# A 7 x 7 convolution by short transforms: the first weight group taken from one copy of the weights, the second copy loaded later

## The chip, the core and the metric

The kernel runs on one core of a Trainium2 chip. The metric is the device time of one execution, in microseconds (us); the smaller the better. The core has five engines, each with its own instruction queue that is worked off in order: TensorE (PE, with weight loads listed apart as PEld), VectorE (DVE), ScalarE (ACT), GpSimd (POOL) and SyncE (SP), which here only issues DMA transfers. Engines wait for each other by semaphores.

## What is computed

A batch of one image of 224 x 224 pixels with 96 channels (bf16) is convolved circularly with a 7 x 7 kernel from 96 to 96 channels. The reference does it by Fourier transforms over the whole image:

```python
def reference(x, w):                      # x (1,224,224,96), w (7,7,96,96), bf16
    wp = jnp.pad(w, ((0, H - K), (0, W - K), (0, 0), (0, 0)))
    Xf = jnp.fft.rfft2(x.astype(jnp.float32), axes=(1, 2))
    Wf = jnp.fft.rfft2(wp.astype(jnp.float32), axes=(0, 1))
    Yf = jnp.einsum('bhwi,hwio->bhwo', Xf, Wf)
    return jnp.fft.irfft2(Yf, s=(H, W), axes=(1, 2)).astype(jnp.bfloat16)
```

## The kernel before

**Tiles and stages.** The height is cut into 8 blocks of 28 rows, the width into 7 tiles of 32 pixels. Along the height a transform with 17 frequencies `s` is used, along the width the seven taps are summed directly. Four kinds of work go through PE:

- pixels: matmuls of a pixel's rows with the transform matrix `Fm` give `xf` (`a_bank`, `f_jobs`). `jit` then makes sums and differences of `xf` on DVE, called `J`, for a group of three frequencies.
- weights: matmuls with the loaded weights `wq` and a selector matrix `Em` give the transformed weights `WF`. `prep_jobs(gi)` returns the jobs of weight group `gi`; group 0 covers the frequencies 0 and 1, group 1 the frequencies 2 to 4, and so on. A group has 12 jobs; each fills one PSUM bank and is evacuated to `WF` by DVE or ACT. From group 1 on, three jobs on DVE follow (`diff`, the difference of two slots of `WF`).
- rounds: `b_round(t, s, ...)` multiplies `xf` and `J` of tile `t` with `WF` at frequency `s`. Two banks, `b0` and `b1`; ACT copies the first into `tt_`, DVE makes `u` and `v`, POOL or DVE adds them into `yf`, which goes to a scratch in DRAM.
- inverse: matmuls with the matrix `G` bring the scratch of a finished tile back to pixels.

**The weights in `wq`.** A row of `wq` is one of the 49 taps, its columns run over input and output channels. A matmul takes every 96th column, so that it sees one output channel `o` for all input channels. Each tap is loaded twice: row 2k holds tap k from column 0, row 2k+1 the same tap shifted by 48 output channels. One matmul over the 98 rows with both halves of `Em` therefore makes the output channels `o` and `o + 48` together. `Em` lies behind the weights in the same tile, and the columns behind it are zeroed by ACT.

**What sets the order.** Every engine's instructions are chained in the order of the program (`_Ordered`), so the source's order is the order of each queue. `evac` gives an evacuation to DVE or ACT by counts of estimated load. All PSUM tiles come from one pool of eight banks (`bank`), reused in turn; PE waits when the bank eight tiles back isn't evacuated. Within the rounds, side jobs (weight groups, pixels) are dealt out by `add(a, b, jobs)`: the jobs are spread over the half rounds a to b - 1, and `pace` runs those that are due in the middle (`mid`) and at the end (`end`) of a round; for the first rounds the middle of round r is half round 2r, the end 2r + 1.

**The start** is written out by hand. SP loads, in this order: the halo pixels of both halves of the image (`xh`, lines 179 to 180), the first half's pixels (`load_x(0, 0)`), the weights in five column pieces of two transfers each (lines 182 to 187), and the second half's pixels, held behind the second piece. PE runs 8 + 9 warm matmuls on zeros, the halos, the first half's pixels, 2 x 11 more warm matmuls, weight group 0, the second half's pixels; then follow `jit(0, 0)` and, with `g_fin()`, the sine that finishes `G`, and round 0. Lines 707 to 717 of it:

```python
    for n in (11, 11):
        warm(n)
    for f in prep_jobs(0):
        f()
    last = [f() for f in fj[0][1]]
    for jg in range(2):
        for d in load_x(1, jg):
            tc.add_manual_dep(d.ins, last[0].ins.name, SYNC, reason="second tile's pixels later")
    for f in jit(0, 0):
        f()
    g_fin()
```

`g_fin` is returned by `build_g(3)`: POOL makes the angles of `G` in a chain of small dependent operations that stands in its queue behind the masks of `Em` and eight memsets, ACT takes the sine (it is the first instruction of ACT behind the pixels' evacuations and ahead of round 0's `tt_`), POOL multiplies.

Of the kernel before, what the change touches and what calls it, by code (L numbers as in the profile page):

```python
# [46 lines left out]
NWC = 5  # L47
HOLD = 2
# [8 lines left out]
def kernel(  # L57
# [15 lines left out]
    PW2 = 2 * PW  # L73
# [81 lines left out]
    wq = wqx[0:PW2]  # L155
    WC = C * C - C2
    Em = wqx[0:PW2, WC:WC + 2 * NSLOT * NTAP].rearrange("p (h a t) -> p h a t", h=2, a=NSLOT)
# [20 lines left out]
    wsrc = w.rearrange("kh kw i o -> (kh kw) (i o)")  # L178
    for jg in range(2):
        load_rows(xh_bufs[jg], jg, W - PAD, PAD)  # L180
    load_x(0, 0)
    wcut = [WC * c // NWC // 128 * 128 for c in range(NWC)] + [WC]
    wdma = []
    for c0, c1 in zip(wcut, wcut[1:]):
        for k, n in ((PW - 1, 1), (0, PW - 1)):
            wdma.append(dma(wqx[2 * k:2 * (k + n), c0:c1],
                bass.AP(wsrc.tensor, wsrc.offset + k * C * C + c0, [[C * C, n], [C2, 2], [1, c1 - c0]])))
    for d in load_x(0, 1):
        tc.add_manual_dep(d.ins, wdma[2 * HOLD + 1].ins.name, SYNC, reason="second pixels behind the weights")

# [9 lines left out]
    warm(9)  # L200
# [19 lines left out]
    zw = wqx[0:PW2, WC + 2 * NSLOT * NTAP:]  # L220
    SE.copy(out=zw, in_=wu[0:PW2, 0:1].to_broadcast(list(zw.shape)))

    nrj = ftile([R, JG]); pw_i = ftile([R, 1]); aa = ftile([R, NS, 2]); phf = ftile([R, NS, 2]); phe = ftile([R, NS, 2])
    twc = ftile([PW2, KT]); mf = ftile([R, JG, NS * 2])
    iota(nrj[:], [[-B, JG]], base=-1, cm=1)
    iota(pw_i[:], [[0, 1]], cm=1)
# [3 lines left out]
    thp = ftile([R, 1]); qq = ftile([R, JG + 1, NS, 2]); fl = ftile([R, JG + 1, NS, 2])  # L230
# [6 lines left out]
    floor_div(VE, thp[:], pw_i[:], 2 * KT)  # L237
# [9 lines left out]
    SE.activation(out=qq[:], in_=qq[:], func=ACTF.Sin, bias=pi_t[:R, :], scale=-2.0 * math.pi / Q)  # L247
# [8 lines left out]
    iota(twc[:], [[1, KT]])  # L256
    pm = ftile([PW2, 1]); twp = ftile([PW2, 1]); hf = ftile([PW2, 1]); mk = ftile([PW2, NTAP]); mk2 = ftile([PW2, 2, NTAP])
    th14 = ftile([PW2, 1])
    GE.tensor_single_scalar(out=th14[:], in_=thp[0:PW2], scalar=-2.0 * KT, op=ALU.mult)
    GE.tensor_tensor(out=pm[:], in0=th14[:], in1=pw_i[0:PW2], op=ALU.add)  # L260
    floor_div(GE, twp[:], pm[:], 2)
    GE.tensor_single_scalar(out=th14[:], in_=twp[:], scalar=-2.0, op=ALU.mult)
    GE.tensor_tensor(out=hf[:], in0=th14[:], in1=pm[:], op=ALU.add)
    GE.tensor_scalar(out=mk[:, 0:KT], in0=twc[:], scalar1=twp[:, 0:1], scalar2=None, op0=ALU.is_equal)
    GE.tensor_tensor(out=mk[:, KT:NTAP], in0=mk[:, 0:6:2], in1=mk[:, 1:6:2], op=ALU.add)
    GE.tensor_scalar(out=mk2[:, 1], in0=mk[:], scalar1=hf[:, 0:1], scalar2=None, op0=ALU.mult)
    GE.tensor_tensor(out=mk2[:, 0], in0=mk[:], in1=mk2[:, 1], op=ALU.subtract)
    for xb in xh_bufs:
        GE.memset(xb[:, PAD * C:], 0.0)
    for xb in x0_bufs + xn_bufs:  # L270
        GE.memset(xb[:, XW:], 0.0)
    for xb in xf_bufs:
        GE.memset(xb[:, :, :, NS - 1, POS - 1, :].rearrange("c p r j -> c (p r) j"), 0.0)

    VE.tensor_tensor(out=Fm.rearrange("p r s j -> p j s r"), in0=qq[:, 0:JG],
                     in1=mf.rearrange("p j (s r) -> p j s r", r=2), op=ALU.mult)
    qe = qq[0:PW2, JG]
    pe3 = ftile([PW2, NSLOT])
# [4 lines left out]
    for r, k in ((0, KT - 1), (1, 0)):  # L283
        VE.tensor_single_scalar(out=pv[:, NS - 2, r:r + 1], in_=thp[0:PW2], scalar=float(k), op=ALU.is_equal)
    VE.tensor_tensor(out=pv[:, :, 2], in0=pv[:, :, 0], in1=pv[:, :, 1], op=ALU.subtract)
    for k0, k1 in ((0, slot(PGRP[0][1], 0)), (slot(PGRP[0][1], 0), NSLOT)):
        VE.tensor_tensor(out=Em[:, :, k0:k1], in0=pe3[:, k0:k1].unsqueeze(1).unsqueeze(3).to_broadcast([PW2, 2, k1 - k0, NTAP]),
                         in1=mk2[:].unsqueeze(2).to_broadcast([PW2, 2, k1 - k0, NTAP]), op=ALU.mult)
# [51 lines left out]
    def prep_jobs(gi):  # L340
# [3 lines left out]
        ncol = (NSLOT_OF(s0, s1) if full else 2 * ns) * NTAP  # L344
# [4 lines left out]
        def mk_(ob):  # L349
            def f():  # L350
                pw = bank()
                pv_ = pw[:, 0:NB * ncol].rearrange("p (k h q) -> p k h q", h=2, q=ncol)
                ev = Em[:, :, slot(s0, 0):slot(s1 - 1, 2) + 1, :]
                ev = ev.rearrange("p h a t -> p h (a t)") if full else ev.rearrange("p h (s r) t -> p h s (r t)", r=3)[:, :, :, 0:2 * NTAP]
                for k in range(hb):
                    o = ob * hb + k
                    TE.matmul(pv_[:, k], lhsT=wqx[0:PW2, o:o + 127 * C + 1:C], rhs=ev, start=True, stop=True)
                pv_ = pv_[0:C]
                o0, o1 = ob * hb, (ob + 1) * hb
                wv = WF[0:C, slot(s0, 0):slot(s1 - 1, 2) + 1]  # L360
                if full:
                    wv = wv.rearrange("i a t (h o) -> i (a t) h o", h=2)
                    apart(("W", gi), ob, evac(wv[..., o0:o1], pv_.rearrange("i k h q -> i q h k"), NB * ncol))
                    return
# [12 lines left out]

    def NSLOT_OF(s0, s1):
        return slot(s1 - 1, 2) + 1 - slot(s0, 0)
# [320 lines left out]
    for jg in range(2):  # L700
        for f in a_bank(0, xf0, xh_bufs[jg], 0, 3, jg, 0):
            f()
# [209 lines left out]
```

## Time and profile before

Three runs gave 269.27, 269.51 and 270.08 us, median 269.51.

| of the profiled execution | |
|---|---|
| span from the first to the last instruction | 267.8 us |
| median of the runs, which includes what lies around the span | 269.51 us |
| PE busy, 0 to 10.96 us | 9.43 of 10.96 us |
| PE busy, 10.96 to 15.71 us | 4.75 of 4.75 us |
| PE busy, 15.71 to 20.23 us | 4.06 of 4.52 us |
| PE busy, 20.23 to 26.64 us | 6.41 of 6.41 us |
| PE busy, 26.64 to 34 us | 7.22 of 7.36 us |
| PE busy, 34 us to the end | 226.50 of 233.80 us |
| granted clock of TensorE | 1.00 in each of these stretches |

How to read the profile: a timeline line has the start in us, the busy time from first to last of the merged instructions in us, the engine, the source line, the operation, what it writes and reads, the shapes, the count, and in brackets the idle time ahead of it with what ended it. Since all calls go through a helper, all instructions of the kernel carry its line, L89, and are told apart by their tiles. Names of buffers stand without numbers; `ct` are the small tables, `pb` a PSUM bank, `wu` the zeros of the warm matmuls. A matmul's time in a group is its latency; what counts in a stream is the distance from start to start.

### The profile page before, as it was taken

The page shows a single profiled execution, that of the slowest core. Times are in us where ns is not written, and L with a number is a line of the kernel's source. Part 1 is how long each engine was busy: PE and PEld are TensorE (multiplying, and loading weights), DVE is VectorE, ACT ScalarE, POOL GpSimd, SP SyncE. Part 2 cuts the span into 40 slices and gives each one's busy share as a digit, 9 for nine tenths or more (in the row PEclk, how much of TensorE's full clock was granted, in tenths as well). Part 3 has the DMA queues.
Part 4 walks back from the last instruction along what each step waited for, and adds up shares of the span by engine and source line. Part 5 has one row for each costly group of instructions (what it writes and reads, how often), then busy time and mean ns, then how long its engine had stood idle before and what let it go on. Part 6 is the DMA issues. An engine that isn't in the chain of part 4 may idle for free. (4 is left out here: it accounts for less than half of the span.)

```text
span 267.8 us, 12172 instructions
## 1 busy us (share of the span) xinstructions
PE 258.4 (96%) x5144; PEld 237.3 (89%) x5144; DVE 214.3 (80%) x457; ACT 194.6 (73%) x483; POOL 98.9 (37%) x156
## 2 busy tenths in 40 slices
PE   8999999999999999999999999999999999999983
PEld 3679999999999999999999998999999889879862
DVE  5658998889899788779787888787898889878624
ACT  5558988587974577988988789887887854278113
POOL 7782315363656435321422222223222342532100
PEclk9999999999999999999999999999999999999999
DMA  6948011811111498997968487979777624887956
GB/s 169 233 130 213 11 47 46 239 48 72 47 47 50 146 266 143 281 272 199 299 170 241 116 221 235 238 204 329 269 148 216 202 98 154 198 229 186 257 115 206
DMA packets 47014, 46.78 MB, mean 175 GB/s; under 512 B 35286, under 2 KB 37986, under 8 KB 46960
## 3 DMA queue, kind: packets, MB, share of 16 engines
q1 hardware_dynamic: 44672, 43.94, 59.3%
q10 hardware_dynamic: 2288, 2.06, 2.6%
q8 instruction: 40, 0.66, 1.0%
q14 instruction: 14, 0.11, 0.2%
HBM read 24.65 MB, written 21.33 MB: 172 GB/s over the span
## 5 line engine op out<-in xcount | busy, mean ns | idle before, releaser
L89 PE MATMUL pb<-WF,J 96*128 96x96 bf16 x2821 | 162.8, 206 | 1.9 <-DVE J L89 1.1
L89 PEld LDWEIGHTS <-J 96*128 96x128 bf16 x2821 | 138.0, 98 | 12.4 <-issue 3.6
L89 POOL TENSOR_TENSOR yf<-v,u 128x384 bf16<-128x384 f32 x79 | 81.4, 1042 | 146.3 <-issue 84.6
L89 ACT CAST xf<-pb 96x408 bf16<-96x408 f32 (+3 forms) x145 | 67.7, 490 | 9.0 <-PE pb L89 5.4
L89 PE MATMUL pb<-WF,xf 96*128 96x96 bf16 x952 | 59.9, 206 | 0.5 <-ACT xf L89 0.5
L89 DVE TENSOR_TENSOR J<-xf 96x1824 bf16<-96x1824 bf16 (+1 forms) x84 | 56.9, 716 | 0.1
L89 PEld LDWEIGHTS <-xf 96*128 96x128 bf16 x952 | 47.0, 98 | 0.7 <-ACT xf L89 0.6
L89 PE MATMUL pb<-Fm,xn 118*128 118x136 bf16 (+3 forms) x640 | 45.5, 199 | 0.2 <-DVE u L89 0.2
L89 PE MATMUL pb<-tt,Gm 102*84 102x384 bf16 (+1 forms) x132 | 32.7, 326 | 0.4 <-ACT J L89 0.3
L89 ACT CAST WF<-pb 96x480 bf16<-96x480 f32 (+1 forms) x59 | 29.1, 578 | 4.8 <-PE pb L89 4.8
L89 PEld LDWEIGHTS <-xn 118*128 118x128 bf16 x640 | 30.3, 97 | 0.3 <-issue 0.3
L89 ACT CAST J<-pb 84x384 bf16<-84x384 f32 (+1 forms) x64 | 27.7, 490 | 2.6 <-PE pb L89 2.6
L89 ACT CAST yo<-pb 84x384 bf16<-84x384 f32 (+1 forms) x63 | 27.1, 486 | 2.3 <-POOL yf L89 1.3
L89 DVE TENSOR_TENSOR J<-J 96x912 bf16<-96x912 bf16 (+2 forms) x42 | 24.2, 577 | 0.0
L89 PE MATMUL pb<-wq 98*128 98x120 bf16 (+1 forms) x288 | 21.3, 226 | 0.0
L89 PEld LDWEIGHTS <-wq 98*128 98x128 bf16 x288 | 19.6, 151 | 0.2 <-issue 0.2
L89 PE MATMUL pb<-wu 128*128 128x512 bf16 (+1 forms) x75 | 16.8, 385 | 1.1 <-DVE ct L89 1.1
L89 PEld LDWEIGHTS <-wu 128*128 128x128 bf16 (+1 forms) x75 | 8.8, 120 | 8.0 <-issue 2.8
L89 DVE TENSOR_TENSOR yf<-v,u 128x384 bf16<-128x384 f32 x26 | 14.9, 572 | 0.9
L89 PEld LDWEIGHTS <-Gm 102*84 102x84 bf16 (+1 forms) x132 | 11.1, 117 | 1.0 <-issue 0.4
L89 ACT COPY xf<-xf 96x816 bf16<-96x816 bf16 (+3 forms) x20 | 11.3, 633 | 0.0
L89 DVE CAST WF<-pb 96x480 bf16<-96x480 f32 (+1 forms) x13 | 7.5, 609 | 4.2 <-PE pb L89 4.2
(386 smaller groups left out, 234.2 us busy)
## 6 DMA issues: line engine op xcount, KB each, us to landing
scr<-yf SPq DMA_DIRECT2D x30, 288.0 KB
xn<-in_x_dram SPq DMA_DIRECT2D x12, 672.0 KB
tt<-scr SPq DMA_DIRECT2D x24, 336.0 KB
out_dram<-yo SPq DMA_DIRECT2D x12, 252.0 KB
out_dram<-J SPq DMA_DIRECT2D x12, 252.0 KB
tt<-scr SPq DMA_DIRECT2D x6, 288.0 KB
WF<-in_x_dram SPq DMA_DIRECT2D x2, 672.0 KB
out_dram<-tt SPq DMA_DIRECT2D x8, 168.0 KB
```

The source lines that it names most:

```text
L89: r = fn(*a, **k)
```

## The change

The two copies of each tap no longer stand in neighbouring rows. The first copy lies in rows 32 to 80, the second (shifted by 48 output channels) in rows 81 to 127 and, its last two taps, in rows 30 and 31. Weight group 0 uses the first copy alone: 96 matmuls over the rows 0 to 80 with 50 columns instead of 48 over 98 rows with 100 columns; the rows 0 to 31 are zeroed for that. Later groups use all 128 rows as before used 98.

- Loads: first half's pixels, tap 48 in two pieces, the other 48 taps of the first copy, halos, second half's pixels, second copy's first 47 rows; its last two rows follow in the queue when group 0 has read the zeros there, and behind them the second tile's pixels.
- PE: 8 + 8 warm matmuls, first half's pixels, 3 warm matmuls, ten of group 0's twelve jobs, halos, second half's pixels, the last two jobs of group 0.
- Zeros: ACT zeroes 1036 f32 columns behind `Em` and, in rows 0 to 31, columns 0 to 1000 and 1000 to 2300; POOL the columns 2300 to 4608 of these rows, behind the masks.
- Masks: VectorE computes the tap and the copy of a row (`hb`, `ha`, `tap`, `hm`), POOL's four operations for them fall away.
- Rounds: group 1's jobs go to the half rounds 1 and 2 (before 0 and 1), the pixel jobs `fj[1][1]` to 0 to 2 (before 1 to 4).

```diff
-NWC = 5
-HOLD = 2
+FILL = 3
+W1 = 32
+W2 = 30
+ZA = 1000
+ZB = 2300
...
-    PW2 = 2 * PW
+    EP = 128
+    K1 = W1 + PW
+    NU = EP - K1
...
+    def load_w(p, k, n, h):
+        m = (C * C, WC)[h]
+        return dma(wqx[p:p + n, 0:m], bass.AP(wsrc.tensor, wsrc.offset + k * C * C + h * C2, [[C * C, n], [1, m]]))
+
+    load_x(0, 0)
+    m = C * C // 16
+    for a, b in ((0, m // 2), (m // 2, m)):
+        dma(wqx[K1 - 1:K1, 0:C * C].rearrange("p (c m) -> p c m", c=16)[:, :, a:b],
+            bass.AP(wsrc.tensor, wsrc.offset + (PW - 1) * C * C + a, [[C * C, 1], [m, 16], [1, b - a]]))
+    load_w(W1, 0, PW - 1, 0)
     for jg in range(2):
         load_rows(xh_bufs[jg], jg, W - PAD, PAD)
-    load_x(0, 0)
-    wcut = [WC * c // NWC // 128 * 128 for c in range(NWC)] + [WC]
-    wdma = []
-    for c0, c1 in zip(wcut, wcut[1:]):
-        for k, n in ((PW - 1, 1), (0, PW - 1)):
-            wdma.append(dma(wqx[2 * k:2 * (k + n), c0:c1],
-                bass.AP(wsrc.tensor, wsrc.offset + k * C * C + c0, [[C * C, n], [C2, 2], [1, c1 - c0]])))
-    for d in load_x(0, 1):
-        tc.add_manual_dep(d.ins, wdma[2 * HOLD + 1].ins.name, SYNC, reason="second pixels behind the weights")
+    load_x(0, 1)
+    load_w(K1, 0, 32, 1)
+    load_w(K1 + 32, 32, NU - 32, 1)
...
     warm(8)
-    warm(9)
+    warm(8)
...
-    SE.copy(out=zw, in_=wu[0:PW2, 0:1].to_broadcast(list(zw.shape)))
+    def zero_a(rows, c0, c1):
+        SE.copy(out=wz[0:rows, c0:c1], in_=zf[0:rows, 0:1].to_broadcast([rows, c1 - c0]))
+    zero_a(EP, WE // 2 + NSLOT * NTAP, 64 * C)
+    zero_a(W1, 0, ZA)
...
+    zero_a(W1, ZA, ZB)
...
+    VE.scalar_tensor_tensor(out=hm[:, 0:1], in0=hb[:], scalar=-2.0, in1=ha[:], op0=ALU.mult, op1=ALU.add)
+    VE.scalar_tensor_tensor(out=hm[:, 1:2], in0=pw_i[:], scalar=float(PW - W1 + W2), in1=hm[:, 0:1], op0=ALU.is_ge, op1=ALU.subtract)
+    for h in range(2):
+        GE.tensor_scalar(out=mk2[:, h], in0=mk[:], scalar1=hm[:, h:h + 1], scalar2=None, op0=ALU.mult)
+    GE.memset(wz[0:W1, ZB:WE // 2], 0.0)
...
+                if full:
+                    pv_ = pw[:, 0:NB * ncol].rearrange("p (k q) -> p k q", q=ncol)
+                    ev = Em[0:K1, 0, slot(s0, 0):slot(s1 - 1, 2) + 1, :].rearrange("p a t -> p (a t)")
+                    o0 = ob * NB
+                    for k in range(NB):
+                        TE.matmul(pv_[:, k], lhsT=wqx[0:K1, o0 + k:o0 + k + 127 * C + 1:C], rhs=ev, start=True, stop=True)
...
     xf0 = new_xf(0)
-    for jg in range(2):
-        for f in a_bank(0, xf0, xh_bufs[jg], 0, 3, jg, 0):
-            f()
     fj = [f_jobs(0, p) for p in range(3)]
     for p in range(3):
         for f in fj[p][0]:
             f()
-    for n in (11, 11):
-        warm(n)
-    for f in prep_jobs(0):
+    warm(FILL)
+    first_w = prep_jobs(0)
+    for f in first_w[:-2]:
         f()
-    last = [f() for f in fj[0][1]]
     for jg in range(2):
-        for d in load_x(1, jg):
-            tc.add_manual_dep(d.ins, last[0].ins.name, SYNC, reason="second tile's pixels later")
+        for f in a_bank(0, xf0, xh_bufs[jg], 0, 3, jg, 0):
+            f()
+    for f in fj[0][1]:
+        f()
+    for f in first_w[-2:]:
+        f()
+    load_w(W2, NU, W1 - W2, 1)
+    for jg in range(2):
+        load_x(1, jg)
...
     for gi in range(1, len(PGRP)):
-        add(2 * PGRP[gi - 1][0], 2 * PGRP[gi - 1][1] - (2 if gi == 1 else 1), prep_jobs(gi))
+        add(2 * PGRP[gi - 1][0] + (gi == 1), 2 * PGRP[gi - 1][1] - 1, prep_jobs(gi))
...
-            add(1, 5, fj[1][1])
+            add(0, 3, fj[1][1])
```

## The prediction

> **What bounds the kernel now.** I read the page's shares and slices first, then the busy time by stretch, then the timeline of the first 27 us on each engine, the waits, and last the order in which the changed program's instructions stand on each engine.
>
> ```profile
> PE 258.4 (96%) x5144; PEld 237.3 (89%) x5144; DVE 214.3 (80%) x457; ACT 194.6 (73%) x483; POOL 98.9 (37%) x156
> ...
> PE   8999999999999999999999999999999999999983
> ```
>
> TensorE is busy 96% of the span, in every slice. In the stretch from 34 us to the end it is busy 226.5 of 233.8 us, so what it loses before 34 us it can hardly win back. But part of its busy time early on is filler:
>
> ```profile
> 10.96 4.91 PE L89 MATMUL pb<-wu 128*128 128x512 bf16 x22
> ...
> 15.71 3.13 PE L89 MATMUL pb<-wq 98*128 98x100 bf16 x48
> ...
> 20.23 0.51 PE L89 MATMUL pb<-WF,xf 96*128 96x96 bf16 x8 [0.46 <-ACT xf L89]
> ```
>
> From 10.96 to 15.7 us PE multiplies zeros while the weights arrive; then come the first weight group (48 matmuls), the second pixels and, at 20.23, round 0. Meanwhile POOL, ACT and DVE do this:
>
> ```profile
> 7.44 0.31 POOL L89 MEMSET WF<- 118x32 bf16 x4
> ...
> 7.94 0.13 POOL L89 IOTA ct<- 102x1 f32 x1
> 8.16 1.75 POOL L89 TENSOR_SCALAR ct<-ct 102x1 f32<-102x1 f32 x4
> ...
> 10.27 1.08 POOL L89 TENSOR_SCALAR ct<-ct 102x1 f32<-102x1 f32 x4
> ...
> 20.47 0.37 POOL L89 TENSOR_TENSOR ct<-ct,ct 102x84 f32<-102x84 f32 x1
> ...
> 20.88 0.37 ACT L89 ACTIVATE ct<-ct,ct 102x84 f32<-102x84 f32 x1 [0.70 <-POOL ct L89]
> 21.15 0.31 ACT L89 COPY tt__556<-pb 128x192 f32<-128x192 f32 x1
> 21.35 4.23 ACT L89 CAST WF<-pb 96x480 bf16<-96x480 f32 x9
> ...
> 25.61 1.79 DVE L89 TENSOR_TENSOR WF<-WF 96x960 bf16<-96x960 bf16 x3 [0.45 <-ACT WF L89]
> ...
> 26.56 0.47 ACT L89 ACTIVATE tt__670<-pb 128x288 f32<-128x288 f32 x1
> ...
> 26.67 0.34 PE L89 MATMUL pb<-WF,J 96*128 96x96 bf16 x4
> ```
>
> POOL builds matrix G in one dependent chain from 7.94 to 20.84 (20.47 + 0.37). ACT needs its result for one sine, which stands in ACT's queue ahead of round 0's copy `tt_`; ACT already waits 0.70 us for it. From there ACT has no idle time up to 34 us: nine evacuations of weight group 1, two halo copies, then round 1's `tt_`. Group 1 is complete at 25.6, and round 2, which multiplies by it, starts at 26.67. So a second chain, POOL to ACT to group 1 to round 2, runs about even with PE. This is the place to watch.
>
> **PE's own sum.** Removed: 1 of 17 first warm matmuls and 19 of 22 later ones, at 4.91/22 = 0.22 us: 4.4 us. Added: 48 matmuls. The 48 with 100 columns took (3.13 - 0.22)/47 = 62 ns each, start to start; the 32 with 120 columns at 20.58 took 2.17 us, or 63 ns. Since 20 more columns cost 1 ns, the weight read (every 96th element, as after the change) sets the pace, so 50 columns also take 62 ns: 48 x 62 = 3.0 us. Bounds: 35 ns, the pace of the 32 second-pixel matmuls (1.10 us), which have contiguous weights, and 65. The new timetable: warm to 6.5; 96 first-pixel matmuls to 9.4 (3.3 us now for 103, less the 7 halo ones); 3 warm to 10.05; 80 of the 96 to 15.05; 12 halo at 0.06 to 15.8; second pixels 1.1 to 16.9; the last 16 to 17.9; evacuation (0.2 + 0.5) to 18.6. Round 0 would start 1.6 us earlier than 20.23.
>
> **Transfers up to there.** First pixels (0.71 MB) and first copy (0.90 MB) are 1.6 MB; by the trace's DMA packets 1.6 MB had come in by 9.0 us. PE asks for them at 10.05, so this is covered by 1 us. Rows are 18 KB instead of 3.6 KB; the packets of 6,144 bytes moved faster (390 GB/s) than those of 3,584 (240), but the one of 16,384 bytes took 1.38 us; at that pace three rows an engine are 4.1 us and the copy lands near 9.5, still in time. Second pixels and the second copy bring 3.4 MB, by 14 to 16 us. SyncE's queue holds each of these until an earlier one has landed, which moves none past that point. The last two rows are new: they wait for the last of the 96 matmuls (17.9), and the second tile's pixels stand behind them. Small transfers took 1.8 to 2.1 us from issue to landing; with 1.38 for the long row up to 3.4: landed at 20.0 to 21.4. Group 1 wants them at about 20.2, so 0 to 1.2 us, if nothing else holds PE. The next pixels are issued at about 18.5 (now 19.72) and are not late.
>
> **POOL and ACT, the step that decides.** Ahead of G's chain POOL loses four one-column operations (5.06 to 6.14: 1.1 us), does four of the short memsets earlier and gains a memset of 32 x 2308 f32. That shape is not in the trace. 136 columns took 0.21 us and 8 took 0.11, so 0.8 ns a column: 2.0 us. Bounds: 1.0 (two columns at once) and 2.6 (held up by DVE). Masks end at 6.6 instead of 7.50, the memset at 8.6, the remaining short ones at 8.85: G starts 0.9 us later. Against that, its first four operations took 1.75 us where four like them took 1.08: DVE was writing the selector matrix (7.54 to 8.93). After the change that write is over by 8.1, so 0.67 comes back: 8.85 + 12.90 - 0.67 = 21.1. If the hold-up falls on the memset, 21.8. I take 21.3, nearer the first because the eight memsets at 7.44 to 7.98 ran beside the same write and stretched to nothing. The bounds: 20.2 to 21.8.
>
> [...]
>
> ACT is free at about 18.2 and then stands still until 21.3, with round 0's `tt_`, two pixel evacuations and six of group 1 behind the sine. PE fills its eight banks and stops too; so the 1.6 us won are spent waiting. Onward: `tt_` starts 0.27 after the sine (20.88 to 21.15 now): 21.57. From there to the end of round 1's `tt_` took 5.88 us (21.15 to 27.03); three fewer evacuations at 4.23/9 = 0.47 and two more of 320 columns at 0.44: 5.35, so 26.9. Now the new serial piece: in the changed order DVE does `u` of round 1 (0.34), which needs that `tt_`, ahead of the last three evacuations of group 1 (0.6 each); before, all three stood ahead of `u`. 26.9 + 0.35 + 1.8 = 29.05, PE starts round 2 at 29.1 instead of 26.67: **2.4 us late**. From there on the two instruction orders differ in a few evacuations up to about round 5 and then not at all, and PE is the bound: I carry all of it.
>
> The other edits (three VectorE operations for the row masks, ACT's zeroing of 1036, 1000 and 1300 columns by 6.0 us at the pace of 2120 in 1.94) lie under the warm matmuls, which end at 6.5; without that cover they would cost some 0.5 us.
>
> **The sum.** The profiled execution spans 267.8 us; the median of runs is 269.51, 1.7 more, which lies around the span. 267.8 + 2.4 = 270.2 profiled; **271.9 us** as a run's time. From the bounds of POOL (-1.1, +0.5), of the carry and of the evacuations (0.5 either way): 270.3 to 273.0 for this case.
>
> **Rivals.**
> Absorbed: after 34 us PE has 7.3 us of gaps, short waits for DVE and ACT; if half the delay vanishes there, +1.2, 270.7. Against it: these waits move with PE.
> Faster, on the other side: the sine does not hold ACT. Then round 0 at 18.6 plus the present 6.44 us from round 0 to round 2 gives 25.0, plus 0.6 for the two late rows 25.6: 1.0 us early, **268.5**. It decides if POOL's result is there by 18.6; that needs G's chain 2.7 us shorter than the rows say. For it: POOL's spans are rough.
> Transfers: the long rows go at half the pace assumed, the two late rows land at 23.5 and group 1 starts after ACT is free: 1.6 more, 273.5. For it: no row of 18 KB is in the trace.
> No effect: the head's gain and the later sine cancel at round 2 because G's chain starts as now; 269.5.
>
> **How the numbers follow.** Forecast 0.62, absorbed 0.14, faster 0.10, transfers 0.08, no effect 0.06. The likeliest is 271.9. The range 269.9 to 273.5 leaves out the faster case, the case of no effect, and 0.04 above. A difference of 0.3% (0.8 us) is about what a measurement of this kernel can tell from none. Slower: forecast, transfers and 0.11 of the absorbed, 0.81; same 0.09; faster 0.10.
>
> **What would show it.** The first weight group starts near 10 us and round 0 near 18.6; ACT idle some 3 us until a sine at 21 to 22; PE idle in several pieces between 19 and 29; round 2 near 29; the 50-column matmuls 62 ns apart. If the sine comes before 19, or round 2 before 26.7, the forecast is wrong.

## The result and the profile after

The changed kernel takes 273.74 us (median of four runs, 272.65 to 274.23), the kernel before 269.47 us (four runs, 269.27 to 270.08): the ratio is 1.0145, with an interval from 1.0117 to 1.0173. The profiled execution spans 272.4 us, 4.6 more than before. The change costs 4.3 us; the forecast was 2.4. (One run of `g1_chunks` below took 641.29 us at a clock of 1.00 and is in no median.)

The page of the changed kernel, busy time and slices:

```profile
PE 261.8 (96%) x5172; PEld 242.3 (89%) x5172; DVE 215.8 (79%) x462; ACT 197.2 (72%) x485; POOL 99.0 (36%) x153
...
PE   8998899999999999999999999999999999999983
...
PEclk9955999999999999999999999999999999999999
```

PE is as busy as before, 96%. New is the row of the granted clock: two slices at 0.5, where the kernel before had 9 throughout. The record of the clock begins at 7.01 us here and at 5.11 us in the kernel before; ahead of it the warm matmuls start 427 ns apart, behind it some 215. So both executions began at half pace, and the 1.00 that the table of the kernel before gives from 0 us on is that of the recorded part. From there on every change of the clock, in every run, lies a whole number of stretches of 3.41 us behind the last (6.83 us are two of them, 13.65 four). Four of them, with the columns PE, PEld, DVE, ACT, POOL (busy us and instructions), granted clock, DMA share and GB/s:

```profile
7.01:10.43 3.42, 3.42 (x102) 2.94 (x101) 3.17 (x6) 2.30 (x5) 2.90 (x12) 1.00 0.95 218
10.43:13.84 3.41, 3.41 (x56) 3.33 (x55) 1.57 (x3) 1.60 (x4) 2.51 (x13) 1.00 1.17 279
13.84:17.25 3.41, 3.41 (x51) 3.41 (x50) 2.27 (x4) 2.03 (x5) 2.74 (x12) 0.50 1.01 118
...
24.08:27.49 3.41, 3.41 (x44) 3.41 (x42) 1.09 (x2) 3.12 (x7) 0.00 (x0) 0.50 0.86 225
```

From 10.43 to 13.84 PE is never idle (3.41 of 3.41 us), but behind the end of the warm matmuls it has only matmuls of 50 columns; then it runs at half clock for 13.65 us, to 27.49. The timeline of the changed kernel, PE from the first weight group to round 2:

```profile
10.63 5.02 PE L95 MATMUL pb<-wq 81*128 81x50 bf16 x80
15.47 2.23 PE L95 MATMUL pb<-Fm,WF 118*128 118x136 bf16 x25
17.97 1.17 PE L95 MATMUL pb<-Fm,WF 118*128 118x64 bf16 x19 [0.27 <-issue]
18.95 1.13 PE L95 MATMUL pb<-wq 81*128 81x50 bf16 x16
20.83 0.80 PE L95 MATMUL pb<-WF,xf 96*128 96x96 bf16 x8 [0.75 <-DVE WF L95]
...
23.63 3.38 PE L95 MATMUL pb<-wq 128*128 128x120 bf16 x32 [0.34 <-DMA wq<-in_w_dram]
...
31.01 0.34 PE L95 MATMUL pb<-WF,J 96*128 96x96 bf16 x4 [0.50 <-DVE WF L95]
```

Round 0 starts at 20.83, not at 18.6; group 1 waits for its weights and starts at 23.63 (before: 20.58); its 32 matmuls take 3.38 us (before 2.17); round 2 starts at 31.01 (before 26.67). ACT and DVE in the same stretch:

```profile
20.80 0.37 ACT L95 ACTIVATE ct<-ct,ct 102x84 f32<-102x84 f32 x1 [0.68 <-POOL ct L95]
21.67 0.32 ACT L95 COPY tt__585<-pb 128x192 f32<-128x192 f32 x1 [0.50 <-PE pb L95]
...
28.90 0.36 DVE L95 SCALAR_TENSOR_TENSOR u<-pb,tt__692 128x192 f32<-128x192 f32 x1 [1.20 <-ACT tt__692 L95]
29.18 1.77 DVE L95 CAST WF<-pb 96x480 bf16<-96x480 f32 x3
```

The sine comes at 20.80, as before (20.88), and round 0's `tt_` waits for PE, not for the sine. `u` does stand ahead of the last three evacuations of group 1, as the forecast said, but PE waits only 0.50 us for them.

How late PE is against the kernel before, taken at the same matmul of the rounds in both traces: 0.6 us at round 0, 4.34 at round 2, 4.41 at 107 us and 4.41 at 248 us. The loss is made between round 0 and round 2 and carried whole to the end. It splits by the rows: group 1 starts 3.05 us later (23.63 against 20.58), and from its start to round 2 it takes 7.38 us instead of 6.09, of which 1.17 are the 32 matmuls at half clock (23.63 to the next matmuls at 26.81, against 20.58 to 22.59). So the first theory was: thin matmuls drop the clock, and the order on DVE costs the rest; its rivals, that the clock is all of it, and that transfers are. A part of round 0's lateness belongs to the execution and not to the change: half pace at the start lasted to 7.01 us here, with the first pixels at 7.44, and in the runs below to between 3.94 (h2_chunks_early, first pixels at 6.24) and 6.85 us (x_pace, 7.36).

### The profile page after: what moved, and what is told of

The parts are those of the page before. It is cut to its first block, busy times and chain, and to the rows that moved or that the text cites. A ratio compares the mean times of both kernels' runs of the same rounds, so it can differ in the third digit from the quotient of the medians.

```text
span 272.4 us, 12227 instructions
## 1 busy us (share of the span) xinstructions
PE 261.8 (96%) x5172; PEld 242.3 (89%) x5172; DVE 215.8 (79%) x462; ACT 197.2 (72%) x485; POOL 99.0 (36%) x153
## 4 chain that ended last, share of the span: by engine, by line
PE 66%; DVE 13%; POOL 7%; issue 6%; DMA 4%; ACT 3%; DVEq 0%; ACTq 0%; POOLq 0%
PE pb L95 66%; POOL ct L95 5%; DVE J L95 4%; DVE WF L95 3%; DVE v L95 3%; DVE u L95 2%; DMA xf<-scrb 2%; ACT xf L95 1%; DMA wq<-in_w_dram 1%; DVE yf L95 1%; DMA scrb<-yf 1%; POOL yf L95 1%; POOL wq L95 1%; ACT J L95 1%; DVE xf L95 0%
## 5 line engine op out<-in xcount | busy, mean ns | idle before, releaser
L95 PE MATMUL pb<-wq 128*128 128x120 bf16 (+1 forms) x336 | 25.4, 234 | 0.3 <-DMA wq<-in_w_dram 0.3
L95 PEld LDWEIGHTS <-wq 128*128 128x128 bf16 (+1 forms) x336 | 23.6, 154 | 0.7 <-issue 0.5
L95 PE MATMUL pb<-wu 128*112 128x384 bf16 (+1 forms) x55 | 13.4, 408 | 1.1 <-DVE ct L95 1.1
L95 PEld LDWEIGHTS <-wu 128*112 128x112 bf16 (+1 forms) x55 | 7.1, 132 | 6.5 <-issue 4.1
```

What stands on the lines that cost most here:

```text
L95: r = fn(*a, **k)
```

## The experiments

All times are medians beside the kernel before on the same chip (269.7 to 269.9 us); "half clock" is the stretch at 0.50 in the profiled execution. The times of the rounds and landings are those of that one execution, in us.

| run | round 0 | last weights of group 1 landed | group 1 | half clock | round 2 | us | ratio (interval) |
|---|---|---|---|---|---|---|---|
| before | 20.23 | 15.43 | 20.58 | none | 26.67 | 269.47 | |
| changed | 20.83 | 23.49 | 23.63 | 13.84-27.49 | 31.01 | 273.74 | 1.0145 (1.0117-1.0173) |
| e1_wide | 21.10 | 23.23 | 23.36 | 19.03-25.86 | 30.43 | 273.25 | 1.0126 (1.0098-1.0155) |
| x_pace | 21.05 | 23.76 | 23.89 | 13.68-27.33 | 31.27 | 274.25 | 1.0168 (1.0145-1.0191) |
| e2_wide_pace | 20.57 | 23.44 | 23.57 | 19.50-26.32 | 30.65 | 272.55 | 1.0111 (1.0086-1.0136) |
| e3_wide_loads | 22.78 | 22.10 | 24.39 | 13.68-20.51 | 31.31 | 275.22 | 1.0197 (1.0172-1.0221) |
| g1_chunks | 18.33 | 20.88 | 21.23 | 22.53-25.94 | 29.61 | 273.41 | 1.0121 (1.0095-1.0147) |
| g2_wide_shift | 20.22 | 23.17 | 23.31 | 21.98-28.80 | 31.07 | 275.61 | 1.0204 (1.0160-1.0249) |
| g3_wide_pace_lsplit | 20.94 | 23.18 | 23.32 | 19.36-26.19 | 30.45 | 273.98 | 1.0151 (1.0121-1.0182) |
| g6_all_parts | 18.69 | 21.99 | 22.54 | 19.77-26.60 | 30.21 | 272.39 | 1.0088 (1.0059-1.0117) |
| h2_chunks_early | 21.64 | 24.51 | 24.75 | 14.18-27.83 | 31.99 | 275.50 | 1.0206 (1.0170-1.0242) |
| h3_chunks_early_pace | 22.00 | 24.38 | 24.62 | 13.55-20.38, 23.79-30.62 | 33.04 | 275.27 | 1.0190 (1.0152-1.0228) |
| h1_all_early | 22.43 | 23.72 | 23.96 | 14.44-21.27, 24.68-28.09 | 31.41 | 274.52 | 1.0187 (1.0130-1.0244) |
| k1_all_act | 19.33 | 21.90 | 22.14 | 23.09-26.50 | 29.57 | 271.64 | 1.0071 (1.0056-1.0085) |

**100 columns (e1_wide).**

```diff
-ev = Em[0:K1, 0, slot(s0, 0):slot(s1 - 1, 2) + 1, :].rearrange("p a t -> p (a t)")
+ev = Em[0:K1, :, slot(s0, 0):slot(s1 - 1, 2) + 1, :].rearrange("p h a t -> p h (a t)")
...
-TE.matmul(pv_[:, k], lhsT=wqx[0:K1, o0 + k:o0 + k + 127 * C + 1:C], rhs=ev, start=True, stop=True)
+TE.matmul(pw[:, k * ncol:(k + 2) * ncol].rearrange("p (h q) -> p h q", h=2), lhsT=wqx[0:K1, o0 + k:o0 + k + 127 * C + 1:C], rhs=ev, start=True, stop=True)
```

> Edit: each of the 96 matmuls of group 0 takes both halves of the tap matrix, 100 columns instead of 50; the 50 extra columns are overwritten by the next matmul (or lie in the bank's unused end), so the result is the changed kernel's. In the changed kernel the 50-column matmuls start 62 ns apart, so PE computes in them less than half of the time; at the end of the 3.4 us stretch that holds nothing else the granted clock falls to 0.50 for 13.65 us. Clock theory: with 100 columns PE is as busy as in the kernel before, the clock stays at 1.00, the first group still takes about 62 ns a matmul (6.0 us), round 0 starts near 19, round 2 near 28.5 (1.85 us behind the kernel before, by a replay of the order on each engine at full clock), and the run takes 271.4 to 271.8 us; of the 4.3 us the clock is about 2.2. Rival A (the clock alone is the whole loss): the clock stays at 1.00 and the run takes 269.0 to 269.9 us. Rival B (the clock falls for the fewer warm matmuls or for the halts of PE, not for the thin matmuls): the clock still falls near 14 us and the run takes 273.5 us or more, since 100 columns cost more at half clock.

The clock now holds through group 0, to 19.03, so the stretch of thin matmuls was what dropped it at 13.84; rival B falls by its condition. But round 0 is no earlier. The timeline of this run, PE:

```profile
14.87 1.25 PE L95 MATMUL pb<-Fm,WF 118*128 118x136 bf16 x25
18.32 0.71 PE L95 MATMUL pb<-Fm,WF 118*128 118x64 bf16 x19 [2.20 <-issue]
18.87 1.48 PE L95 MATMUL pb<-wq 81*128 81x100 bf16 x16
```

PE stands for 2.2 us in the middle of the second pixels, between two matmuls that wait for no semaphore; the pixels had landed at 14.1. This was in neither theory. In the changed kernel the same place costs 0.3 us (the 0.27 above). PE's instructions 447 and 449 stand on the two sides of the halt in the changed kernel, in this run and in the three others with its transfers and its instruction numbers (x_pace, e2, g3), and the trace's transfer records suggest why: one queue, marked as instructions, moves 40 blocks of 16,384 B beside PE's 10,379 instructions, about one per 256. They follow PE's instructions 192, 448, 704 and so on: in the changed kernel each of the 40 begins between 0.25 us ahead of its own and 5.12 us behind it, in the kernel before between 0.40 ahead and 3.51 behind. From that I take them for blocks of 256 of PE's instructions, and these numbers for the borders. After PE passed the border at instruction 192 (9.53 us in the changed kernel) the transfer of the next block began only at 14.63 and ended at 16.07; PE went on at 17.97. In the kernel before, the same transfer began 1.6 us after the border. In between stand the packets of the weights: those of 18,432 B took 1.26 us in the median, the later ones of 18,336 B up to 3.2. The wide matmuls only bring PE to the border earlier. In the six halts of this kind (g2_wide_shift below included) PE went on 1.6 to 2.2 us after the end of the transfer. Rival A falls, and so does the sum of the clock theory.

**The old dealing-out (x_pace), and both (e2_wide_pace).**

```diff
-add(2 * PGRP[gi - 1][0] + (gi == 1), 2 * PGRP[gi - 1][1] - 1, prep_jobs(gi))
+add(2 * PGRP[gi - 1][0], 2 * PGRP[gi - 1][1] - (2 if gi == 1 else 1), prep_jobs(gi))
...
-add(0, 3, fj[1][1])
+add(1, 5, fj[1][1])
```

> Edit: the changed kernel with the dealing-out of the kernel before: group 1 dealt from half round 0 (not 1) to one half round earlier, the filters of its second block (the halves of fj that read it) into half rounds 1 to 5 (not 0 to 3); nothing else. Order theory (part of the loss is the vector engine's sums of round 1 standing ahead of the last evacuations of group 1 that round 2 waits for): at the fallen clock round 2 starts about 1 us sooner than in the changed kernel, near 30.0, and the run takes 272.6 to 273.0 us. Rival (the dealing-out moves nothing, round 2 waits for the 32 weight matmuls at half clock and for the two late rows): round 2 stays within 0.3 us of 31.0 and the run at 273.5 to 274.0 us. The clock falls as in the changed kernel by both.

> Edit: 100 columns in group 0's matmuls and the dealing-out of the kernel before together. Clock theory with the order theory: clock 1.00, round 2 near 27.6 (0.96 us behind the kernel before by the replay), run 270.3 to 270.7 us. Rival A (clock alone): same as with 100 columns alone, 269.0 to 269.9 us. Rival (order moves nothing): same as with 100 columns alone, whatever that is, within 0.3 us.

Measured 274.25 and 272.55 us: the order theory's gain of 1 us did not come in the first, round 2 is 0.26 later. The timeline of the run of both, PE:

```profile
20.57 0.80 PE L95 MATMUL pb<-WF,xf 96*128 96x96 bf16 x8 [0.75 <-DVE WF L95]
23.57 3.18 PE L95 MATMUL pb<-wq 128*128 128x120 bf16 x32 [2.20 <-DMA wq<-in_w_dram]
```

With the old order group 1's turn comes right after round 0, and it waits 2.20 us for the two late rows. The new order fills that time with other work and then pays at DVE. Either way group 1 starts when the rows are there. But round 2 is not the end of it: with the old order PE makes up 0.7 to 0.8 us behind round 2 (x_pace is 4.60 late there and 3.84 at 248 us, e2_wide_pace 3.98 and 3.27), with the new one nothing. In the medians the order is worth 0.7 us between e1_wide and e2_wide_pace and -0.5 between the changed kernel and x_pace; the intervals overlap in both pairs, so its worth stays open.

**Transfers (e3_wide_loads).**

```diff
-return dma(wqx[p:p + n, 0:m], bass.AP(wsrc.tensor, wsrc.offset + k * C * C + h * C2, [[C * C, n], [1, m]]))
+return dma(wqx[p:p + n, 0:m].rearrange("p (c m) -> p c m", c=3),
+           bass.AP(wsrc.tensor, wsrc.offset + k * C * C + h * C2, [[C * C, n], [m // 3, 3], [1, m // 3]]))
...
 load_w(W1, 0, PW - 1, 0)
+load_w(W2, NU, W1 - W2, 1)
...
-zero_a(W1, 0, ZA)
+zero_a(W2, 0, ZA)
...
-load_w(W2, NU, W1 - W2, 1)
 for jg in range(2):
     load_x(1, jg)
```

> Edit: 100 columns in group 0's matmuls, and the loads of the weights changed: each row of w that is 18 KB long moved as three pieces of 6 KB, and the last two rows of the second copy loaded with the others, behind the first copy, to rows that no zero and no matmul of group 0 touches (so two rows fewer are zeroed over the first copy's width, and the two late transfers of the changed kernel are gone). Transfer theory (rows of 18 KB move slower, 14.7 B/ns on each DMA engine against 24 for pieces of 6 KB, and group 1 waits for the late rows): the first copy lands near 9.0 instead of 10.25, the second by 15.5 instead of 18.85 to 21.1, no wait of group 1 for weights; round 0 near 18, and round 2 0 to 1 us sooner than with 100 columns alone. Order theory: the earlier rounds only stand longer at the vector engine's queue, round 2 stays near 28.9 (2.3 us behind the kernel before by the replay), run 271.7 to 272.1 us, no sooner than with 100 columns alone.

Measured 275.22 us. The experiment does not answer its question, but for reasons that teach. The three pieces are contiguous on both sides, and the packets stayed at 18,432 and 18,336 B. And group 0 does read the two rows (against zeros of the tap matrix), so it waited until they landed at 11.86: it started at 12.00, the stretch to 13.68 was poor in matmuls, the clock fell, and round 0 came at 22.78. It also shows the halt at the next border: the next block began to come 5.4 us after PE passed instruction 448, and PE stood 0.65 us between the instructions 704 and 705, at 27.3 us.

**Packets of 6 KB (g1_chunks).**

```diff
-return dma(wqx[p:p + n, 0:m], bass.AP(wsrc.tensor, wsrc.offset + k * C * C + h * C2, [[C * C, n], [1, m]]))
+for a, b in zip(range(0, m, m // 3), range(m // 3, m + 1, m // 3)):
+    dma(wqx[p:p + n, a:b], bass.AP(wsrc.tensor, wsrc.offset + k * C * C + h * C2 + a, [[C * C, n], [1, b - a]]))
```

> Edit: the changed kernel with both copies of the weights (and the two late rows) each moved by three transfers of a third of the columns, so that a packet has 6,144 or 6,112 B instead of 18,432 or 18,336; nothing else. New theory, from the runs with 100 columns: PE halts without a wait between its instructions 447 and 449 in every run, and its instruction blocks of 16,384 B are fetched in between (the fetch begins 5.1 us after PE passes the block border, at 14.6 us, and PE goes on 1.9 us after its end, at 18.0), because the fetch stands behind packets of 18 KB that take 1.25 to 3.2 us each. With packets of 6 KB the fetch begins within 2.5 us (as in the kernel before, 1.6 us), PE does not halt there, and the two late rows land by 22.3 instead of 23.5. The clock still falls near 14 us (thin matmuls), so the run gains only part: 272.8 to 273.5 us. Rival (the length of packets plays no part, the fetch waits for the amount in the queues): the fetch still begins near 14.6 and the run takes 273.5 to 274.2 us.

With the same amount in shorter packets the block of instructions begins to come 2.7 us after the border instead of 5.1, and PE does not stop there. Round 0 starts at 18.33, where the prediction had put it. The run gains 0.33 us all the same, less than these intervals can tell. (Its 273.41 us lie in the range of the new theory, but the clock did not fall near 14 us, which that range had in it.) PE, ACT, POOL and DVE of this run:

```profile
18.33 0.50 PE L95 MATMUL pb<-WF,xf 96*128 96x96 bf16 x8 [0.76 <-DVE WF L95]
...
21.23 1.19 PE L95 MATMUL pb<-wq 128*128 128x120 bf16 x16 [1.16 <-DMA wq<-in_w_dram]
...
29.61 0.34 PE L95 MATMUL pb<-WF,J 96*128 96x96 bf16 x4 [1.17 <-DVE WF L95]
...
22.06 0.37 ACT L95 ACTIVATE ct<-ct,ct 102x84 f32<-102x84 f32 x1 [4.38 <-POOL ct L95]
...
17.46 2.13 POOL L95 TENSOR_SCALAR ct<-ct,ct,ct 102x84 f32<-102x84 f32 x2
...
18.11 1.36 DVE L95 TENSOR_TENSOR J<-xf 96x1824 bf16<-96x1824 bf16 x2
...
27.50 0.36 DVE L95 SCALAR_TENSOR_TENSOR u<-pb,tt__700 128x192 f32<-128x192 f32 x1 [2.38 <-ACT tt__700 L95]
27.78 1.77 DVE L95 CAST WF<-pb 96x480 bf16<-96x480 f32 x3
```

The links of the forecast's chain are all there: round 0 at 18.3, ACT standing 4.38 us for the sine, `u` ahead of three evacuations, PE waiting 1.17 us for them, round 2 at 29.61. But this run also has group 1 waiting 1.16 us for the two late rows and the clock at 0.50 from 22.53 to 25.94, so round 2 at 29.61 does not measure the chain alone. The clock stayed at 1.00 to 22.53 with 50-column matmuls: here no stretch of 3.41 us held them alone (below).

And the sine is later than in the changed kernel, 22.06 against 20.80, outside the forecast's 20.2 to 21.8. The same two operations of POOL took there:

```profile
17.38 1.06 POOL L95 TENSOR_SCALAR ct<-ct,ct,ct 102x84 f32<-102x84 f32 x2
```

With round 0 early, DVE makes the sums `J` while POOL's chain still runs: of the two operations the one that starts at 18.11 us, together with the first `J`, took 1.48 us instead of 0.41. The same shows in e2_wide_pace (1.23 instead of 0.36, sine at 21.70) and in g2_wide_shift (1.40 instead of 0.42, sine at 22.02). In the changed kernel `J` starts at 20.61, when POOL is at the chain's last operation, and nothing is stretched. So a part of what an earlier round 0 wins is lost on POOL, a collision that the forecast did not have.

**The border moved (g2_wide_shift).** With the 100 columns, and 48 one-column matmuls in place of four of the first warm ones, which moves every later instruction by 88.

```diff
 warm(8)
-warm(8)
+pwt = bank()
+for _ in range(4):
+    TE.matmul(pwt[:].rearrange("p (a b) -> p a b", a=4), lhsT=wu[:, 0:128], rhs=wur, start=True, stop=True)
+for i in range(48):
+    TE.matmul(pwt[0:1, i:i + 1], lhsT=wu[:, 0:1], rhs=wu[:, 0:1], start=True, stop=True)
```

> Edit: 100 columns in group 0's matmuls, and of the second eight matmuls that only keep PE busy four replaced by 48 matmuls of one row and one column (on zeros, read by nobody), so that the border of PE's instruction block comes 88 instructions sooner (between the 80th-last and the last matmuls of group 0's first part instead of in the second pixels); transfers as in the changed kernel. Fetch theory: the block is asked for at about 8 us, before the queues hold the second pixels and the second copy, PE does not stand from 15.9 to 18.3 as with 100 columns alone, round 0 starts at 18.7 to 19.2 instead of 21.1 (unless a halt shows at the new border, near 13.5), the clock stays at 1.00 until 20 us at least, and with the late rows issued 2 us sooner round 2 starts 1 to 2 us sooner: run 271.2 to 272.3 us. Rival (PE waited for something else there, the second pixels or a bank): PE stands at the same matmul to 18.3, run 273.0 to 273.6 us.

In the second pixels PE no longer stops; it stops at the 64th matmul of group 0, which is now instruction 450. The timeline of this run:

```profile
10.93 4.02 PE L95 MATMUL pb<-wq 81*128 81x100 bf16 x63
15.57 1.25 PE L95 MATMUL pb<-wq 81*128 81x100 bf16 x17 [0.61 <-issue]
...
23.31 3.39 PE L95 MATMUL pb<-wq 128*128 128x120 bf16 x32 [1.39 <-DMA wq<-in_w_dram]
```

The halt goes with the instruction's number, not with the work, which fits the border of a block; that PE waits for the transfer itself is inferred from the times. The time (275.61) was expected to fall and rose. The first pixels started at 7.55 because PE waited 0.58 us for them, and round 0 moved only to 20.22; of the 1.9 us more than the changed kernel little is made at the start: at 248 us PE is 4.63 us late here and 4.41 there, and the rest of the 1.1 us between the two profiled executions comes behind that.

**Late rows in 32 pieces (g3_wide_pace_lsplit), and all parts (g6_all_parts).**

```diff
-load_w(W2, NU, W1 - W2, 1)
+m = WC // 8
+for a, b in ((0, m // 2), (m // 2, m)):
+    lw = dma(wqx[W2:W1, 0:WC].rearrange("p (c m) -> p c m", c=8)[:, :, a:b],
+        bass.AP(wsrc.tensor, wsrc.offset + NU * C * C + C2 + a, [[C * C, W1 - W2], [m, 8], [1, b - a]]))
...
```

g6 joins this to the 100 columns, the old dealing-out and the packets of 6 KB, and moves the sine:

```diff
-g_fin()
 stmp_cm.__exit__(None, None, None)
...
+if r == 6:
+    g_fin()
```

> Edit: 100 columns and the dealing-out of the kernel before, as in the run of the two together (272.55 us), and the two late rows moved in 32 pieces of 1,146 B by two transfers instead of two packets of 18 KB. Late-row theory (with the old dealing-out group 1 waited 2.2 us for these two rows, to 23.57): they land near 22.2, PE starts group 1 by 22.4 and round 2 at 29.4 to 29.7 instead of 30.65, run 271.3 to 271.8 us. Rival (the 15 rows in front of them are what is late, they landed at 20.8, and at half clock the 32 matmuls take the time back): run 272.2 to 272.6 us.

> Edit: all four together, and the sine moved: 100 columns in group 0; the dealing-out of the kernel before; weights in packets of 6 KB; the two late rows in 32 pieces; and the tables of the angles kept in tiles of their own, so that their sine on the scalar engine can be called six rounds later and the buffers of the rounds do not wait for POOL's chain. If the clock, the fetch, the late rows, the order and the sine are the whole loss: clock 1.00 throughout, round 0 at 18.5 to 19.0, group 1 by 21, round 2 at 25.5 to 26.7 and the run 267.5 to 269.5 us, at or below the kernel before. If transfers as such (the second pixels ahead of the second copy) still bind: 270 to 271 us.

The pieces brought the rows from issue to landing in 2.8 us instead of 3.5 (e2_wide_pace: 19.98 to 23.44), but PE had reached the end of group 0 later: they landed at 23.18, 0.26 sooner, and the run of 273.98 shows no gain. With all parts round 0 is at 18.69 and the sine out of the way, and PE then does almost nothing for 3.35 us. The timeline of that run:

```profile
18.69 0.50 PE L95 MATMUL pb<-WF,xf 96*128 96x96 bf16 x8 [0.76 <-DVE WF L95]
22.54 3.38 PE L95 MATMUL pb<-wq 128*128 128x120 bf16 x32 [3.35 <-DMA wq<-in_w_dram]
```

The expected 267.5 to 269.5 us did not come; 272.39 is 1.3 us better than the changed kernel, with intervals that touch, and the wait of 3.35 us is for transfers.

**The two rows early (h2, h3, h1).** All three have the packets of 6 KB; the two rows are loaded in 32 pieces ahead of the first copy and rows 0 to 29 alone are zeroed over the weights' width; h3 adds the old dealing-out, h1 also the 100 columns and the late sine.

```diff
+m = WC // 8
+for a, b in ((0, m // 2), (m // 2, m)):
+    lw = dma(wqx[W2:W1, 0:WC].rearrange("p (c m) -> p c m", c=8)[:, :, a:b],
+        bass.AP(wsrc.tensor, wsrc.offset + NU * C * C + C2 + a, [[C * C, W1 - W2], [m, 8], [1, b - a]]))
...
 load_w(W1, 0, PW - 1, 0)
...
-zero_a(W1, 0, ZA)
+zero_a(W2, 0, ZA)
...
-load_w(W2, NU, W1 - W2, 1)
```

> Edit: the changed kernel with packets of 6 KB, and the last two rows of the second copy (tile rows 30 and 31) loaded at the start, in 32 pieces ahead of the first copy, to rows that are then not zeroed (group 0 reads them against zeros of the tap matrix), so that group 1 waits for nothing that starts only after group 0. With packets of 6 KB alone group 1 waited 1.16 us for these rows, to 21.23, and round 2 came at 29.61. Late-row theory: group 1 starts when the rest of the second copy has landed, near 20.2, its 32 matmuls run at full clock, and round 2 comes at 27.0 to 28.0, run 271.0 to 272.0 us. Order theory (the forecast's: the vector engine's sums of round 1 stand ahead of the last evacuations of group 1): round 2 stays at 28.4 to 29.3 with PE waiting over 0.8 us for an evacuation on the vector engine just before it, run 272.2 to 273.1 us.

> Edit: the last one with the dealing-out of the kernel before (group 1 from half round 0, the second pixels' second block in half rounds 1 to 5). Order theory: no evacuation of group 1 is left behind round 1's sums, round 2 comes 0.8 to 1.5 us sooner than in the last one, near 27.5, run 270.8 to 271.6 us. Rival (the order costs nothing once the rows are there in time): within 0.3 us of the last one. [...]

> Edit: all parts: packets of 6 KB, the two rows early, the old dealing-out, 100 columns in group 0, and the sine of the angles six rounds later with its tables in tiles of their own. Against the last one it differs by the 100 columns and the sine. Sine theory (POOL's chain ends at 20.8 and the scalar engine stands still till then, with round 0 at 18.5): round 1 and 2 come 0.8 to 2 us sooner than in the last one, round 2 at 26.0 to 27.0, run 269.2 to 270.4 us, near the kernel before. Rival (the sine lies beside other waits): within 0.4 us of the last one.

All three medians lie above the changed kernel's (for h1 and h3 within the intervals), and they are inconclusive on the order and the sine. Two more transfers at the front of SP's queue made the third part of the first copy wait for an earlier landing, as SP's ninth transfer did in the changed kernel (issued at 5.43 us; the first had landed at 5.41): it was issued at 5.5 us instead of 4.0 (h2), landed at 11.8 instead of 9.9, and group 0 started at 11.88, after 2.30 us in which PE did nothing; the second copy slid by more, its first 47 rows from 20.03 (g1_chunks) to 24.51.

**The two rows early by ACT's queue (k1_all_act).** As h1, with the two rows' transfers issued by ACT, so that SP's order is that of g6, and four filler matmuls behind group 0.

```diff
-    lw = dma(wqx[W2:W1, 0:WC].rearrange("p (c m) -> p c m", c=8)[:, :, a:b],
+    lw = SE.dma_start(out=wqx[W2:W1, 0:WC].rearrange("p (c m) -> p c m", c=8)[:, :, a:b],
...
 for f in first_w[-2:]:
     f()
+warm(4)
```

> Edit: the run of all parts with the late rows in 32 pieces (272.39 us; group 1 waited 3.35 us for them, to 22.54, and the clock was at 0.50 from 19.77 to 26.60) with two differences: the two rows are moved at the start by the scalar engine's queue, so that the order of SP's transfers and their semaphores is the one of that run (in the runs with the rows early, SP moved them, and the third part of the first copy was issued 1.4 to 2.2 us later, so group 0 started at 11.5 to 12.2); and four matmuls of 512 columns on zeros are put behind group 0, where PE stands for 0.9 us. Each has its own sign in the trace. Late-row theory: group 0 starts at 10.0 to 10.5 and group 1 at 20.0 to 20.8, when the second copy has landed. Clock theory: the stretch from 16.4 to 19.8 is filled to 0.6, no half clock up to 23, and the first 32 matmuls of group 1 take 2.2 us instead of 3.4. Both: round 2 at 26.4 to 27.5 instead of 30.2 and the run at 268.7 to 269.8 us, level with the kernel before. Late rows alone (clock falls all the same): 270.0 to 270.8. Neither (the loss lies in the transfers of the second copy as a whole): 271.5 us or more.

271.64 us, the best of the variants and still 0.71% above the kernel before. Its timeline, PE, and one stretch of its windows (columns as above):

```profile
18.42 1.03 PE L95 MATMUL pb<-wu 128*128 128x512 bf16 x4
19.33 0.50 PE L95 MATMUL pb<-WF,xf 96*128 96x96 bf16 x8
22.14 2.81 PE L95 MATMUL pb<-wq 128*128 128x120 bf16 x32 [2.31 <-DMA wq<-in_w_dram]
```

```profile
19.68:23.09 3.41, 1.10 (x20) 0.99 (x18) 1.29 (x3) 0.81 (x3) 1.85 (x3) 1.00 1.00 227
```

The clock holds past 19.7, after a stretch with 0.84 of the columns of a full one; without the filler's 0.25 it would be 0.59, so whether the filler did it is not shown. It falls at 23.09, after a stretch with 1.10 us of PE. Group 1 still waits 2.31 us, although the two rows are long there: the 47 other rows of the second copy land at 21.9, behind the second pixels (15.9) and beside the next tile's pixels, which SP now issues at 15.9. So the two rows were only the last of a late copy, the third case of the expectation. To put the second copy ahead of the second pixels was not tried.

**What the runs say together.** In the changed kernel and in every run but e3_wide_loads, group 1 started 0.1 to 0.6 us after its last weights landed. Before, they lay ready for 5.15 us. Whatever was taken away in front of that point (half clock, halts, order, sine) was given back there: round 0 moved between 18.3 and 22.8 us and round 2 only between 29.6 and 33.0, never to 26.7. That group 1 waits for the second copy is read from the rows of all these runs. That the loss would go with that wait is argued and not shown: no run had the second copy there by 20.6 us and a clean start.

## Why the prediction was right and wrong

**PE's own sum.** The price was right: 80 matmuls of 50 columns in 5.02 us, 61 ns from start to start, and the same at half clock. Group 0 began at 10.63 instead of 10.05, because half pace at the start lasted to 7.01 us in this execution. Round 0 did not begin at 18.6 but at 20.83: a halo and second-pixel stretch costed at 1.8 us took 3.5 (15.47 to 18.95), at half clock and with the halt of 0.27 us. That the timetable was right for a full clock is shown by g1_chunks, 18.33. The prediction carried the clock of 1.00 over without a word.

**Transfers, the step that was mis-sized.** The forecast's sum has nothing for them, and the two late rows are only in its rivals. The prediction said of the two late rows: "landed at 20.0 to 21.4. Group 1 wants them at about 20.2, so 0 to 1.2 us", and of second pixels and second copy, that they come "by 14 to 16 us". The second copy's first 47 rows landed at 21.12, the two rows at 23.49. Issue to landing was within the bound (20.24 to 23.49, 3.25 us against 3.4); the issue was some 2 us later than assumed, because group 0 ended later. In place of 0 to 1.2 us stand 3.05 us of a later group 1, and 1.17 us for its matmuls at half clock, of the 4.34 at round 2. That the 1.9 us by which round 2 missed the forecast (31.01 against 29.1) lie near the 2.2 by which round 0 missed it proves no cause: with round 0 on time (g1_chunks) the run was no faster beyond what can be measured.

**POOL and ACT.** The prediction called this the step that decides; in the changed kernel it did not. The memset took 2.01 us (estimate 2.0); G's chain started at 8.59 instead of 8.85, and the sine came at 20.80, not 21.3. In the changed kernel it holds nobody up, since round 0 is later still: the sign that the prediction named, ACT idle some 3 us until a sine at 21 to 22, did not come (0.68 us). In g1_chunks it held ACT for 4.38 us, with the sine at 22.06 after the collision with `J` (1.48 us for an operation of 0.41).

**Round 2.** The order on DVE is as read from the instruction lists, and with round 0 on time PE does wait there (1.17 us in g1_chunks); that round 2 at 29.61 is so near the forecast's 29.1 is in part chance, since late rows and half clock are in it too. In the changed kernel the order is the second in line and shows 0.50 us.

**The carry** was right for the changed kernel: 4.34 us at round 2, 4.41 at 248 us; "absorbed" falls.

**The rivals.** "Transfers" named the two rows at 23.5 and 273.5 us, which is what came, though not by its reason alone: the two rows started late more than they moved slowly, while the second copy in front of them did move slowly, with packets of up to 3.2 us. "Faster" had as its condition that the sine does not hold ACT; in g6_all_parts it does not, and the run is slower than before. "No effect" falls. The direction was right; the size was 4.3 instead of 2.4. That the range reaches up to the measured time (273.5; measured 273.74, as a ratio 1.0148 and 1.0145) it owes to that rival and not to the chain that was summed: the forecast lies near by luck.

## What to carry to other kernels

A transfer that is moved behind others is costed by when its last row lands against when it is wanted, and by what it is issued behind; bytes over a mean rate said 16 us where 21 to 23.5 came. When matmuls get narrower, count columns in each stretch of 3.4 us and not PE's busy share alone: here PE was busy for 3.41 of 3.41 us, with 2,700 columns where the filler had 8,192, and the clock fell. When a stage is moved forward, ask what it will then run beside: in g1_chunks `J` came to lie on POOL's chain and stretched it by 1.1 us. And when the measured loss equals the lateness of one event, undo that event before believing it: here it was given back at the next wait.

## What the hardware showed unexpectedly

- **The clock fell under a dense stream of 50-column matmuls.** A stretch of 3.41 us full of 512-column filler held 8,192 columns in the kernel before (11.94 to 15.35 us). Against that the changed kernel's stretch before the fall (10.43 to 13.84) held 2,700 (0.33), without a gap of PE: it was busy for 3.41 of 3.41 us. Over the first 30 us of all runs, of 14 stretches at full clock with at most 0.40, 13 were followed by half clock; of those above 0.40 all but two (0.48 in g2_wide_shift, 0.57 in h1_all_early) kept it. No sharp bound is shown, and some matmul records are missing.
- **PE stood where a block of its instructions came late.** With 18 KB packets the transfer of the block after instruction 192 began 4.2 to 6.1 us after the border in the changed kernel and five runs (3.5 in e3_wide_loads), with 6 KB packets 1.1 to 2.9 us after it; one block later the runs with the rows early had 3 to 4 us with 6 KB packets too, without a halt, so the length of the packets alone does not set it. That a block is asked for at the border, and that PE stands for it, is inferred: in the changed kernel the four blocks from 27 to 45 us, when the queues are light, begin within 0.3 us of it, later ones up to 3 us after it.
- **Long packets were only a little slower per byte here:** 18,432 B took 1.26 us in the median (14.6 B/ns, changed kernel), 6,144 B 0.36 us (17 B/ns, g1_chunks, the pixels' packets of this size included). The first copy landed at 9.71 us with the long and at 9.87 us with the short ones: what differed with the short ones is when the block of instructions began to come, 2.7 us after the border instead of 5.1.
- **Half clock did not slow the 50-column matmuls** of the changed kernel (61 ns from start to start at 1.00 and at 0.50), but the 120-column ones: 99 ns instead of 63.
- **POOL took longer beside DVE's `J`:** beside the 1.1 us of the first `J`, one operation of POOL took 1.48 us instead of 0.41 (g1_chunks), 1.40 instead of 0.42 (g2_wide_shift) and 1.23 instead of 0.36 (e2_wide_pace).
